# A fused attention and feed-forward kernel: the first pair's squares moved to ACT and DVE, the second pair's moments split, the first weight transfer tied to the first scale

## The chip, the cores and the metric

One core of one Trainium2 chip. The metric is the device time of one execution in microseconds (us). TensorE is written PE, VectorE DVE, ScalarE ACT, GpSimd POOL, SyncE SP. The "span" of a trace is the time from its first to its last event; it is some 1.8 us shorter than the timed figure of the same execution.

## The reference, cut to what matters

```python
q_n = q / (norm(q) + 1e-6); k_n = k / (norm(k) + 1e-6)   # 8 batches, 12 heads, 448 x 64, fp32
attn = softmax(q_n @ k_n.T / 0.1)
x = (attn @ v)                                           # regrouped to 3584 x 768
h = x @ w_in                                             # W1: 768 x 2048
out = (h * cos(h)) @ w_out                               # W2: 2048 x 768
```

## The kernel before

Work runs in pairs of heads, six pairs to a batch; pairs and batches are counted from 1 here. For each pair: load q and k; get the row norms; scale; transpose on PE and copy (DVE); scores (PE); exponentials (ACT, four of 896 columns); products with the values (PE). After six pairs the first projection, cosine (ACT), product (DVE) and second projection follow. The program is recorded operation by operation, a list scheduler gives each engine an order, and semaphores are put in afterwards. So a small edit can move many instructions.

The row norms come in two ways. Letters in `PLAN["sq"]`, one entry for each of the first six pairs, choose:

```python
PLAN = {
    "sq": ["BA", "BA", "P", "BP", "P", "P"],   # B: moments on DVE, mended by A(CT) or P(OOL)
    "scale": ["DD", "P", "P", "P", "P", "P"],  # without B: squares, by the named engine(s)
}
...
    BEHIND = ("sq0.2", "sq0.2")
...
            if how[0] == "B":
                moments(u, p, how)        # 16 bn_stats of 64 columns, a mend, a short row sum (L752)
            else:
                square(u, p, how, heads)  # ACT (L728), DVE (L730) or POOL (L732), to bf16
                reduce(u, p, heads)       # one row sum of 1024 columns on DVE (L761)
            rnorm(u, p, p + 1)            # ln and exp on ACT (L789, L792)
            scale(u, p, PLAN["scale"][UP * u + p])   # L800
...
    load_w1(0)                            # POOL issues the two halves of W1: the transfer casts
    load_w1(1)
...
    for x, y in enumerate(BEHIND):
        P.order_only(find(y), find("W1.%d" % x))
```

Labels read `sq0.2` = squares of group 0 (six heads), third pair. Two buffers each hold six heads of q and k (`raw`) and of v (`vin`); loads for a later group wait until an earlier group's scales or copies have freed the buffer. The third group's loads (heads 1 to 6 of the second batch, pairs 7 to 9) go out in this way between 11 and 17 us in the kernel before, the fourth group's at 37, the fifth's (heads 1 to 6 of the third batch) at 57. The texts on record of the experiments count heads from 0 ("heads 6 to 11" are heads 7 to 12 here), their "second batch's last query" is that of the third group, and they call the cosine a sine.

## Time and profile before

| | |
|---|---|
| time, three executions | 427.87 us median, 427.61 to 428.27 |
| span of the trace | 424.1 us |
| first exponential; 13th; end of the 24th | 12.60; 24.64; 34.49 us |
| first cosine of the first batch | 40.04 us |
| W1, first half: issue, landing | 9.89, 26.85 us |

The stretches 8 to 14, 15 to 25 and 25 to 40 us of the kernel before (columns: stretch, its length, then busy time and instruction count of PE, PEld, DVE, ACT, POOL, then clock, DMA share and GB/s):

```profile
8.00:14.00 6.00, 5.14 (x33) 2.20 (x32) 5.84 (x17) 2.08 (x7) 4.89 (x4) 1.00 1.12 293
15.00:25.00 10.00, 8.82 (x121) 4.93 (x118) 8.07 (x16) 9.64 (x17) 9.77 (x8) 1.00 1.12 236
25.00:40.00 15.00, 14.87 (x212) 9.44 (x210) 12.94 (x55) 10.77 (x13) 6.13 (x11) 1.00 1.13 229
```

Two things are to be seen. The last column is never low: the DMA engines are full (the column before it, their share, stands at 1.12 to 1.13), at 293 GB/s with loads alone and at some 235 with W1 beside them. And PE, which is what bounds the kernel (busy for 416.4 of 424.1 us), is idle for only 0.13 us of 15 from 25 us on.

### The profile page before, as it was taken

Reading aid. Unit: us, or ns where it says so; the run is one execution under the profiler, and the core shown is the slowest. Engines: PE = TensorE matmul, PEld = TensorE weight load, DVE = VectorE, ACT = ScalarE, POOL = GpSimd, SP = SyncE. Lnnn points to the kernel's source line nnn. Section 1 sums busy time; section 2 is a strip of 40 time slices with the busy share of each in tenths; the row PEclk is TensorE's granted clock in tenths of the full one; section 3 lists DMA queues with packets and bytes.
Section 4 is the critical chain, followed back from the end, with each engine's and each line's share of the span. In section 5 each row is a group of like instructions: output and inputs, shape, how many; then the busy total and the mean of one; then the engine's idle time right before and its main releaser. Section 6 shows DMA issues by size and latency. Waiting matters only on the chain.

```text
span 424.1 us, 8975 instructions
## 1 busy us (share of the span) xinstructions
PE 416.4 (98%) x3794; PEld 230.6 (54%) x3794; DVE 221.9 (52%) x403; ACT 259.4 (61%) x316; POOL 194.5 (46%) x147
## 2 busy tenths in 40 slices
PE   8899999999999999999999999999999999999997
PEld 3356555555555555555555555555555555555555
DVE  6978876465626359224663358434582344234422
ACT  2895498874777557674577547775567745754400
POOL 3872589645575556925277055751369100000000
PEclk9999999999999999999999999999999999999999
DMA  8999997496299794779529791388935501220033
GB/s 238 262 234 227 241 260 174 97 265 178 72 219 218 170 250 108 137 133 276 135 65 160 192 273 49 82 158 207 195 87 130 121 0 36 64 60 0 2 91 97
DMA packets 92008, 63.19 MB, mean 149 GB/s; under 512 B 52288, under 2 KB 86976, under 8 KB 91968
## 3 DMA queue, kind: packets, MB, share of 16 engines
q1 hardware_dynamic: 87312, 55.47, 56.4%
q0 software_dynamic: 3680, 6.29, 8.0%
q10 hardware_dynamic: 976, 0.86, 0.7%
q8 instruction: 30, 0.49, 0.5%
q14 instruction: 10, 0.08, 0.1%
HBM read 45.61 MB, written 11.01 MB: 134 GB/s over the span
## 4 chain that ended last, share of the span: by engine, by line
PE 85%; ACT 10%; DVE 2%; DMA 1%; POOL 1%; issue 1%; ACTq 0%; POOLq 0%
PE PP L979 28%; PE SC L924 25%; PE AV L873 11%; PE AV L924 9%; ACT PX L855 6%; PE SC L850 5%; PE AV L850 3%; ACT L645 2%; ACT cosb L944 2%; PE SC L979 1%; PE AV L979 1%; DVE st L741 1%; DMA raw<-in_k_dram 1%; DVE qks L800 1%; PE PP L903 1%; PE PP L924 1%
## 5 line engine op out<-in xcount | busy, mean ns | idle before, releaser
L979 PE MATMUL PP<-W,gT 128*128 128x384 bf16 x832 | 152.3, 327 | 0.0
L855 ACT ACTIVATE PX<-SC 112x896 bf16<-112x896 f32 x144 | 123.3, 916 | 2.4 <-PE SC L850 2.2
L732 POOL TENSOR_TENSOR sq<-raw 112x1024 bf16<-112x1024 f32 x39 | 73.2, 1893 | 87.8 <-DMA raw<-in_q_dram 58.9
L924 PE MATMUL SC<-xT,W 128*128 128x448 bf16 x552 | 109.0, 353 | 0.4 <-DVE rcp L883 0.4
L979 PEld LDWEIGHTS PP<-W,gT 128*128 128x128 bf16 x832 | 74.2, 98 | 61.6 <-issue 18.7
L800 POOL TENSOR_TENSOR qks<-raw,rn 112x1024 bf16<-112x1024 f32 x47 | 88.1, 1901 | 8.2 <-ACT rn L792 7.9
L944 ACT ACTIVATE cosb<-SC,cst 128x896 f32<-128x896 f32 x46 | 46.2, 1007 | 58.0 <-PE SC L924 55.4
L946 DVE TENSOR_TENSOR gT<-SC,cosb 128x896 bf16<-128x896 f32 x46 | 50.1, 1091 | 57.2 <-ACT cosb L944 57.1
L924 PEld LDWEIGHTS SC<-xT,W 128*128 128x128 bf16 x552 | 53.3, 98 | 49.2 <-issue 0.5
L855 ACT ACTIVATE PX<-AV 112x896 bf16<-112x896 f32 x48 | 44.0, 917 | 48.9 <-PE AV L850 48.9
L873 PEld LDWEIGHTS AV<-va,PX 112*128 112x128 bf16 x1536 | 49.6, 97 | 14.6 <-ACT PX L855 11.4
L873 PE MATMUL AV<-va,PX 112*128 112x65 bf16 x1536 | 56.0, 194 | 0.5
L988 DVE COPY osb<-PP 128x384 f32<-128x384 f32 x52 | 28.8, 554 | 46.3 <-PE PP L979 46.3
L761 DVE TENSOR_REDUCE n<-sq 112x16 f32<-112x1024 bf16 x42 | 50.0, 1210 | 1.5 <-POOL sq L732 1.5
L850 PE MATMUL SC<-qkT 64*128 64x448 bf16 x288 | 43.0, 353 | 1.8 <-DVE qkT L840 0.7
L924 PE MATMUL AV<-xT,W 128*128 128x448 bf16 x204 | 41.5, 353 | 0.0
L883 DVE RECIPROCAL rcp<-AV 112x8 f32<-112x8 f32 x48 | 9.9, 205 | 56.4 <-PE AV L873 56.3
L884 DVE TENSOR_TENSOR xs<-AV,rcp 112x512 bf16<-112x512 f32 x48 | 33.2, 691 | 2.1
L710 POOL CAST va<-vin 112x1536 bf16<-112x1536 f32 x14 | 20.4, 1463 | 27.5 <-PE AV L873 19.5
L924 PEld LDWEIGHTS AV<-xT,W 128*128 128x128 bf16 x204 | 19.9, 98 | 18.5
L944 ACT ACTIVATE cosb<-AV,cst 128x896 f32<-128x896 f32 x17 | 17.1, 1007 | 20.3 <-PE AV L924 20.2
L946 DVE TENSOR_TENSOR gT<-AV,cosb 128x896 bf16<-128x896 f32 x17 | 18.5, 1089 | 15.8 <-ACT cosb L944 15.6
(54 smaller groups left out, 184.7 us busy)
## 6 DMA issues: line engine op xcount, KB each, us to landing
vin<-in_v_dram SPq DMA_DIRECT2D x16, 672.0 KB, 9.1
raw<-in_k_dram SPq DMA_DIRECT2D x12, 672.0 KB, 7.6
raw<-in_q_dram SPq DMA_DIRECT2D x12, 672.0 KB, 9.3
W<-in_moe_w_in_dram POOLq DMA_DIRECT2D x2, 1536.0 KB, 21.4
W<-in_moe_w_out_dram POOLq DMA_DIRECT2D x4, 768.0 KB, 21.3
raw<-in_k_dram SPq DMA_DIRECT2D x12, 224.0 KB, 7.0
out_dram<-osb SPq DMA_DIRECT2D x7, 336.0 KB, 2.8
out_dram<-osb SPq DMA_DIRECT2D x8, 288.0 KB, 3.1
```

Source lines behind the costliest of these rows:

```text
L732: pool(lambda e, x=x, y=y: e.tensor_tensor(y, x, x, ALU.mult), src_, dst, 0.1 + n * 1.78e-3, label=name)
L761: dve(lambda e, o=o, hs=hs: e.tensor_reduce(out=n2v[i][:, o, :], in_=sqv[p][:, hs[0] : hs[-1] + 1, :, :], axis=mybir.AxisListType.X, op=AL ...
L800: f = lambda e, s0=s0, s1=s1: e.tensor_tensor(qksv[i][:, p, s0:s1, :, :].rearrange("p s h d -> p h s d"), rawv[i][:, h, s0:s1, :], bass.AP ...
L850: t = e.matmul(bank[:, a, 0:S], qkT[k].ap()[r, NP * c : NP * c + 128], qkT[k].ap()[r, S : 2 * S], start=True, stop=True)
L855: act(lambda e: e.activation(PXv[j][:, c, 0 : 2 * S].rearrange("p (a s) -> p a s", a=2), bank[0:NP, :, 0:S], ACT.Exp, scale=1.0 / TAU), [n ...
L873: t = e.matmul(AVv[:, a, DV * x : DV * x + n], PXv[j][:, c, k : k + 128], vav[i][:, NJ * (2 * p + a) + c, 0:n], start=(c == 0), stop=(c == ...
L884: dve(lambda e: e.tensor_tensor(xsv[y].rearrange("p x h d -> p h x d"), AXv[:, :, :, 0:D], bass.AP(rcp[y], 0, [[NS, NP], [NJ, 2], [1, NJ], ...
L924: t = e.matmul(ph[:, a, 0:S], W1v[:, c, 128 * n : 128 * n + 128], xTv[b % 2][:, c, :], start=(c == 0), stop=(c == NKC - 1))
L944: act(lambda e, ph=ph, cz=cz: e.activation(cosv[cz], ph[:, :, 0:S], ACT.Sin, bias=cst.ap()[:, 0:1], scale=1.0), names(gi) + ["cst0"], [("c ...
L946: dve(lambda e, ph=ph, cz=cz, gi=gi: e.tensor_tensor(gTv[:, 2 * gi : 2 * gi + 2, S * (b % 2) : S * (b % 2) + S], ph[:, :, 0:S], cosv[cz], ...
L979: r = e.matmul(po[:, 0 : w1 - w0], gTv[:, y, col : col + 128], W2v[:, y, w0:w1], start=(y == 0), stop=(y == NF - 1))
L988: dve(lambda e, po=po, o=o, w0=w0, w1=w1: e.tensor_copy(osb[o].ap()[:, w0:w1], po[:, 0 : w1 - w0]), keys, [("osb", o, w0)], w1 - w0, label ...
```

## The change

The intent is an earlier first exponential: the first pair's norm should come sooner, and POOL should be silent while DVE scales that pair.

```diff
-    "sq": ["BA", "BA", "P", "BP", "P", "P"],
+    "sq": ["AD", "BA", "P", "BP", "P", "P"],
...
-    BEHIND = ("sq0.2", "sq0.2")
+    BEHIND = ('scale0.0', 'scale0.0')
...
     P.order_only(find("scale0.0"), find("red0.1"))
+    P.order_only(find("red0.0"), [o for o in P.ops if o.label == "bn0.1"][0])
+    P.order_only(find("qkT0"), find("bn0.1"))
...
-        P.order_only(find(y), find("W1.%d" % x))
+        y = find(y)
+        (P.order_only if y.eng == "POOL" else after)(*((y, find("W1.%d" % x)) if y.eng == "POOL" else (find("W1.%d" % x), y)))
...
+    P.order_only(find("X16"), find("load v u7"))
```

In what the scheduler makes of it, W1's first half goes out on POOL directly behind DVE's scales and ahead of pair 3's square; the second half goes out much later, behind pair 4's scale.

## The prediction

> **What bounds the kernel now.** I read the page first, then the chain of work that ended last in order of time, then the timelines of ScalarE (ACT), GpSimd (POOL) and VectorE (DVE) for the first 36 us, and the landing times of the first loads.
>
> The page's busy rows say that TensorE has nothing left over the whole span:
>
> ```profile
> PE 416.4 (98%) x3794; PEld 230.6 (54%) x3794; DVE 221.9 (52%) x403; ACT 259.4 (61%) x316; POOL 194.5 (46%) x147
> ```
>
> A change on DVE and POOL can therefore only win where the chain isn't on PE, and that is the start. The chain in order of time, cut to the start (start us, us, what):
>
> ```profile
> 0.74 3.37 DMA raw<-in_k_dram
> ...
> 4.14 3.14 DVE st L741 x24
> 7.28 0.12 DVE n L752
> 7.39 1.02 DVE st L741 x8
> 8.42 2.69 DVE qks L800 x2
> ...
> 12.84 1.91 POOL qks L800
> ...
> 24.73 3.23 ACT PX L855 x4
> 27.97 0.04 issue
> 28.01 0.36 PE SC L850 x2
> ...
> 33.80 1.62 PE SC L924 x8
> ```
>
> Up to 12.6 us the chain is the first pair's work: load k, moments (L741), row sums, scale (L800). From 12.6 to 28 it alternates between POOL's scale of the next pairs and ACT's exponentials (PX); from 28.01 on it is PE without holes, through the first projection (L924 from 33.80). So the change has to be priced by when ACT's 24 exponentials of the first six pairs run. ACT's timeline (start, us, engine, line, what):
>
> ```profile
> 12.60 0.92 ACT L855 ACTIVATE PX<-SC 112x896 bf16<-112x896 f32 x1
> 13.41 0.30 ACT L789 ACTIVATE lnn<-n,cst 112x16 f32<-112x16 f32 x1
> 13.74 0.21 ACT L792 ACTIVATE rn<-lnn 112x16 f32<-112x16 f32 x1
> 13.86 3.62 ACT L855 ACTIVATE PX<-SC 112x896 bf16<-112x896 f32 x4
> ...
> 24.18 0.31 ACT L789 ACTIVATE lnn<-n,cst 112x16 f32<-112x16 f32 x1
> 24.52 0.21 ACT L792 ACTIVATE rn<-lnn 112x16 f32<-112x16 f32 x1
> 24.64 9.85 ACT L855 ACTIVATE PX<-SC 112x896 bf16<-112x896 f32 x12
> ```
>
> ACT is full from 12.60 to 34.49: 24 exponentials at 9.85/12 = 0.82 us and four pairs of small ln/exp of about 0.5 us. What feeds them comes from POOL, which has one hole of 1.05 us, before 12.84:
>
> ```profile
> 8.05 1.89 POOL L732 TENSOR_TENSOR sq<-raw 112x1024 bf16<-112x1024 f32 x1 [6.57 <-DMA raw<-in_q_dram]
> 9.89 1.90 POOL L1012 DMA_DIRECT2D W<-in_moe_w_in_dram  x2
> 12.84 3.76 POOL L800 TENSOR_TENSOR qks<-raw,rn 112x1024 bf16<-112x1024 f32 x2 [1.05 <-ACT rn L792]
> ```
>
> And the first pair's two scales on DVE, minimum/median/maximum in ns:
>
> ```profile
> L800 DVE TENSOR_TENSOR qks<-raw,rn x2: 676/1416/2156, 8.3 to 10.4; 112x512 bf16<-112x512 f32 x2
> ```
>
> Two equal instructions, 2.16 and 0.68 us: the long one started at 8.34, inside POOL's square (8.05 to 9.94), and ended 0.56 us after it.
>
> [...] a 1024-column square takes 1.08 us here. [...] here W1's first half lands 17.0 us after its issue.
>
> **The change, part by part.** Pairs are counted from 1.
>
> *Pair 1's squares.* Removed: 16 DVE moment instructions (0.127 us from start to start), ACT's fix of the moments (0.25) and a row sum of 0.20. Added: one ACT square of 512 columns[...], one DVE square of 512 columns (0.68, the free L800) and one row sum over 1024 (1.21, the L761 row). k lands at 4.12 and q at 4.38 (3.4 and 3.6 us after issue). DVE squares 4.41 to 5.09[...], the row sum runs 5.11 to 6.32. Before, the row sum ended at 7.40, because k of pair 2 was put in front of it. ln and exp (0.31 + 0.21 + hand-overs) give the norm at 6.9 in place of 7.98. Eight moments of pair 2, now ordered behind the row sum, hold DVE until 7.3; so the scales start at 7.3, not 8.34: 1.0 us won.
>
> *The first W1 issue now waits for the scale.* It stands ahead of pair 3's square in POOL's order, so POOL is silent while DVE scales: 0.68 + 0.60 to 8.55, where before it was 11.10. [...] In all 2.5 us are won on pair 1's scale.
>
> *Pair 2's moments split around the copies.* The q half (1.0 us) now stands between the two copies of pair 1's transposes, so the second copy ends at 10.2 (before 11.95) and the first exponential can start at about 10.9: 1.7 us won.
>
> *What gives it back.* In the changed order POOL does, one after the other from 8.65: issue W1 (1.06), square pair 3 (1.89, to 11.6), scale pair 2, scale pair 3. DVE's row sum of pair 3 (1.21) cannot end before 12.8, and ACT, which works in order, has pair 3's ln and exp directly behind the first exponential. The second exponential then starts at 12.85 + 0.55 = 13.4, where before it was 13.86. ACT stands idle 1.0 us and only 0.45 of the 1.7 stay. Next gate: the scales of pairs 2 and 3 end at 11.6 + 3.75 = 15.35 (before 16.6), the moment fix of pair 4 at 16.0, its norm at 16.75. With that norm out of the way the second exponential of pair 2 starts at 17.55, before 18.08: 0.5. Last gate: POOL squares pair 5 (17.85), scales pair 4 (19.7), issues the second W1 (20.65, this one came before everything else until now), squares pair 6 (22.5); row sum to 23.75, norm to 24.25. ACT reaches this point at 23.7. The twelve last exponentials start at 24.25, before 24.64: 0.4.
>
> *Sum.* The exponentials end 0.4 us earlier, PE behind them the same, since its order from the first projection on is the old one but for one matmul moved forward. No later term of the diff adds work. 427.87 - 0.4, so 427.4.
>
> **The rivals.** *A: the whole 1.7 us arrive.* [...] Against it: POOL carries the same 17.5 us of work from 8.05 to 26.66 with a hole of 1.05; it now starts 0.6 later, so it can't finish pair 6's scale much earlier than now. If ACT's wait on pair 3 is shorter than I think, 426.2. *B: W1 or W2 arrive late.* The second W1 issue moves from 10.9 to 19.7. Against it: the first half lands at 26.8 now and the second queues behind it on the same queue; it is first needed at 43.98, and lands at 36.7 today. W2's last quarter is tighter: landing 57.4, and PE waited 0.2 us for it. If that transfer doesn't move forward, it takes back some 0.2 of the 0.4; with a real delay the time is 427.9 to 428.5. *C: the rearranged order of later batches costs or wins something.* The scheduler has moved a few score and output matmuls between 55 and 120 us. PE is full there, so I give it 0.3 us either way.
>
> **Range and chances.** The middle is 0.4 us won. The lower end, 426.3, is rival A nearly whole; the upper end, 428.2, is the gain eaten by B and C. Two per cent would be 8.6 us, five times the whole idle start that the change touches, and a loss of that size would need a weight transfer late by as much. Faster or slower by 2%: 1% each.
>
> **What would show it.** Right, step by step: both DVE scales of pair 1 near 0.68 us and over by about 8.6; the first exponential at 10.9 and a hole of about 1 us on ACT behind it, ended by pair 3's row sum; the second exponential near 13.4; the twelve last exponentials from about 24.25; the first long run of L924 near 33.4. Wrong: no hole behind the first exponential (then rival A), a PE wait for W at 44 or 57 us that grows (rival B), or a start that is 0.4 earlier at 34 us and an end that isn't (rival C).

The sum of the prediction was 427.87 − 0.4, so 427.4 us. Two of its terms are cut: the time of ACT's 512-column square of pair 1 and its end (nothing hung on it; in the trace of after it took 0.63 us), and the mechanism to which the 1.5 us of the first scale was put down. The 1.5 us itself is measured, 2.16 less 0.68 in the trace of before, and with the 1.0 us of the earlier start it makes the 2.5 that the text goes on with (8.55 against 11.10); that the 1.5 would go was the author's estimate.

## More of the kernel before

DVE's timeline of before in the stretch that will matter (start, us, engine, line, what):

```profile
35.97 1.10 DVE L741 BATCH_NORM_STATS2 st<-raw 112x6 f32<-112x64 f32 x8
36.98 0.19 DVE L883 RECIPROCAL rcp<-AV 112x8 f32<-112x8 f32 x1
37.21 0.69 DVE L884 TENSOR_TENSOR xs<-AV,rcp 112x512 bf16<-112x512 f32 x1
37.82 1.10 DVE L741 BATCH_NORM_STATS2 st<-raw 112x6 f32<-112x64 f32 x8
```

The second batch's moments (L741) stand between the row scales of the first batch's output (L884), in order, with no idle time in square brackets: their loads are just there. The landing of the values of heads 7 to 12, one of the loads that W1 meets (the row, then issue to landing):

```profile
L698 SPq DMA_DIRECT2D vin<-in_v_dram x1: 1347/1347/1347, 6.6 to 6.6; - x1
...
DMA to landing us min/median/max: 12.6/12.6/12.6
```

## The result and the profile after

| | before | after |
|---|---|---|
| time, median (range), 6 executions each | 428.07 us (426.40 to 429.09) | 428.30 us (427.27 to 429.25) |
| span of the trace | 424.1 | 426.3 |
| ratio after/before, 95% interval | | 1.0008, 0.9984 to 1.0032 |

A ratio here is the mean time of one kernel's fast runs over that of the other's of the same rounds, so it is not quite the ratio of the medians quoted. The 428.30 lies 0.1 us above the range that was predicted, and 0.9 above its middle.

The busy row of the page after hardly differs from that of before:

```profile
PE 416.3 (98%) x3790; PEld 229.7 (54%) x3790; DVE 220.4 (52%) x388; ACT 260.1 (61%) x316; POOL 194.7 (46%) x147
```

The front is as it was meant to be. First pair 1's scales, from the view of that line, then ACT's timeline:

```profile
L800 DVE TENSOR_TENSOR qks<-raw,rn x2: 674/679/684, 7.7 to 8.2; 112x512 bf16<-112x512 f32 x2
```

```profile
11.28 0.90 ACT L855 ACTIVATE PX<-SC 112x896 bf16<-112x896 f32 x1
12.93 0.31 ACT L789 ACTIVATE lnn<-n,cst 112x16 f32<-112x16 f32 x1 [0.75 <-DVE n L761]
13.26 0.22 ACT L792 ACTIVATE rn<-lnn 112x16 f32<-112x16 f32 x1
13.39 2.51 ACT L855 ACTIVATE PX<-SC 112x896 bf16<-112x896 f32 x3
...
24.44 3.32 ACT L855 ACTIVATE PX<-SC 112x896 bf16<-112x896 f32 x4
27.96 6.69 ACT L855 ACTIVATE PX<-SC 112x896 bf16<-112x896 f32 x8 [0.20 <-PE SC L850]
...
41.86 1.01 ACT L944 ACTIVATE cosb<-SC,cst 128x896 f32<-128x896 f32 x1 [5.90 <-PE SC L924]
```

Both scales take 0.68 us; the first exponential starts at 11.28 (before 12.60); the hole behind it is 0.75 us and is ended by pair 3's row sum; the 13th exponential starts at 24.44 (before 24.64). But then there is a new wait for PE of 0.20: the 17th exponential, the first of pair 5, starts at 27.96, as in before (24.64 and four steps of 0.82, about 27.9). The 24th exponential ends at 34.65 (before 34.49), and the first cosine comes at 41.86, 1.8 us later than before. PE's holes after 26 us name the place:

```profile
31.41 0.37 PE L903 MATMUL PP<-ident,xs 112*128 112x112 bf16 x4 [0.25 <-DVE xT L907]
39.96 0.37 PE L903 MATMUL PP<-ident,xs 112*128 112x112 bf16 x4 [1.09 <-DVE xs L884]
```

Before has no such line between 26 and 44 us. DVE, which PE waits for, waits for loads (compare the four lines of before):

```profile
32.34 1.11 DVE L741 BATCH_NORM_STATS2 st<-raw 112x6 f32<-112x64 f32 x8 [0.98 <-DMA raw<-in_q_dram]
...
37.95 1.11 DVE L741 BATCH_NORM_STATS2 st<-raw 112x6 f32<-112x64 f32 x8 [1.50 <-DMA raw<-in_q_dram]
...
39.21 0.69 DVE L884 TENSOR_TENSOR xs<-AV,rcp 112x512 bf16<-112x512 f32 x1
...
42.90 1.11 DVE L741 BATCH_NORM_STATS2 st<-raw 112x6 f32<-112x64 f32 x8 [1.00 <-DMA raw<-in_q_dram]
```

And the chain of work that leads to the fifth group's loads, in order of time, answers the chain shown for before, which had no transfer in it after the first load (the chains of two later traces of before do hold one each, of 28.86 us of W2 and of 11.95 us of q, so this is no mark of the kernel):

```profile
18.05 1.87 POOL qks L800
19.93 2.19 SPq L686
22.12 0.04 issue
22.16 20.71 DMA raw<-in_q_dram
42.88 0.02 issue
42.90 0.05 DVE st L741
...
54.85 3.77 POOL qks L800 x2
...
59.07 10.90 DMA raw<-in_q_dram
```

One q load of the second batch takes 20.7 us; DVE's moments, POOL's norms and scales and the next load hang on it. The values of heads 7 to 12 show the same:

```profile
L698 SPq DMA_DIRECT2D vin<-in_v_dram x1: 1283/1283/1283, 7.0 to 7.0; - x1
...
DMA to landing us min/median/max: 19.3/19.3/19.3
```

19.3 us from issue to landing in place of 12.6. Two causes are possible: W1's first packet moves at 14.81 us rather than 15.37, ahead of more of these loads; or the loads of this one execution were slow from the start, as the stretch 8 to 14 us suggests (before: 293 GB/s):

```profile
8.00:14.00 6.00, 4.67 (x34) 1.87 (x33) 5.68 (x25) 2.62 (x7) 5.27 (x4) 1.00 1.13 259
25.00:40.00 15.00, 13.56 (x198) 8.23 (x197) 11.36 (x46) 10.74 (x13) 7.47 (x18) 1.00 1.12 236
```

### The profile page after: what moved, and what is told of

It is laid out like the page before. It is cut to its first block, busy times and chain, and to the rows that moved or that the text cites. A ratio compares the mean times of both kernels' runs of the same rounds, so it can differ in the third digit from the quotient of the medians.

```text
span 426.3 us, 8957 instructions
## 1 busy us (share of the span) xinstructions
PE 416.3 (98%) x3790; PEld 229.7 (54%) x3790; DVE 220.4 (52%) x388; ACT 260.1 (61%) x316; POOL 194.7 (46%) x147
## 4 chain that ended last, share of the span: by engine, by line
PE 76%; DMA 7%; ACT 7%; POOL 4%; issue 2%; DVE 2%; SPq 1%; ACTq 0%; POOLq 0%; DVEq 0%
PE PP L979 26%; PE SC L924 22%; PE AV L873 10%; PE AV L924 8%; DMA raw<-in_q_dram 7%; PE SC L850 4%; ACT PX L855 3%; PE AV L850 3%; ACT L645 2%; POOL qks L800 2%; ACT cosb L944 2%; PE SC L979 1%; PE AV L979 1%; DVE gT L946 1%; POOL sq L732 1%
## 5 line engine op out<-in xcount | busy, mean ns | idle before, releaser
L924 PE MATMUL SC<-xT,W 128*128 128x448 bf16 x552 | 109.0, 352 | 0.2 <-DVE xT L907 0.2
L924 PEld LDWEIGHTS SC<-xT,W 128*128 128x128 bf16 x552 | 53.3, 98 | 49.1 <-DVE xT L907 0.6
L873 PEld LDWEIGHTS AV<-va,PX 112*128 112x128 bf16 x1536 | 49.5, 97 | 14.9 <-ACT PX L855 11.4
L873 PE MATMUL AV<-va,PX 112*128 112x65 bf16 x1536 | 55.7, 193 | 0.6
L761 DVE TENSOR_REDUCE n<-sq 112x16 f32<-112x1024 bf16 x43 | 51.2, 1211 | 2.9 <-POOL sq L732 2.4
L924 PE MATMUL AV<-xT,W 128*128 128x448 bf16 x204 | 41.5, 352 | 0.0
L710 POOL CAST va<-vin 112x1536 bf16<-112x1536 f32 x14 | 20.5, 1465 | 23.4 <-PE AV L873 19.4
L924 PEld LDWEIGHTS AV<-xT,W 128*128 128x128 bf16 x204 | 19.9, 98 | 18.5
L944 ACT ACTIVATE cosb<-AV,cst 128x896 f32<-128x896 f32 x17 | 17.1, 1008 | 19.4 <-PE AV L924 19.3
## 6 DMA issues: line engine op xcount, KB each, us to landing
W<-in_moe_w_in_dram POOLq DMA_DIRECT2D x2, 1536.0 KB, 17.1
```

The costliest lines, as they stand in the source:

```text
L761: dve(lambda e, o=o, hs=hs: e.tensor_reduce(out=n2v[i][:, o, :], in_=sqv[p][:, hs[0] : hs[-1] + 1, :, :], axis=mybir.AxisListType.X, op=AL ...
L873: t = e.matmul(AVv[:, a, DV * x : DV * x + n], PXv[j][:, c, k : k + 128], vav[i][:, NJ * (2 * p + a) + c, 0:n], start=(c == 0), stop=(c == ...
L924: t = e.matmul(ph[:, a, 0:S], W1v[:, c, 128 * n : 128 * n + 128], xTv[b % 2][:, c, :], start=(c == 0), stop=(c == NKC - 1))
L944: act(lambda e, ph=ph, cz=cz: e.activation(cosv[cz], ph[:, :, 0:S], ACT.Sin, bias=cst.ap()[:, 0:1], scale=1.0), names(gi) + ["cst0"], [("c ...
```

## The experiments

Eighteen runs were made, some of unchanged kernels. **Theory 1**: the change's early start of W1 takes bandwidth of the DMA from the loads that DVE needs next, and so takes back the gain of the front. **Theory 2**: the front's gain is lost whatever W1 does, because PE or POOL have no room behind it. **Theory 3**: what differs is the execution, not the kernel.

In some experiments ("frozen order") the scheduler is not asked again: an operation is put directly behind another in the finished order, and all else keeps its place.

```python
    P.arrange()
    def ops(label): return [o for o in P.ops if o.label == label]
    def put(o, y, later=1e-4): o.start = y.start + later
```

n1 and n2, whose front starts later, are not in the table. Read its columns so: q1, GB/s of the loads from 8 to 14 us (the queue of SP and ACT alone, counted in the trace's packet records; in f3 W1 is already under way in this stretch); W, first packet of W1; v, landing of the values of heads 7 to 12; q2, landing of the last q of the third group; E, end of the 24th exponential; cos, first cosine; S − E, span less E; q3, landing of the fifth group's q.

| run | q1 | W | v | q2 | E | cos | q3 | span | S − E |
|---|---|---|---|---|---|---|---|---|---|
| before | 293 | 15.4 | 19.2 | 37.8 | 34.5 | 40.0 | 67.6 | 424.1 | 389.6 |
| r1_before_again | 281 | 15.3 | 20.8 | 38.4 | 34.4 | 39.9 | 67.7 | 424.2 | 389.8 |
| t1_before | 251 | 16.3 | 23.1 | 40.6 | 34.7 | 40.3 | 69.4 | 426.3 | 391.6 |
| after | 259 | 14.8 | 26.3 | 42.9 | 34.7 | 41.9 | 70.0 | 426.3 | 391.6 |
| r2_after_again | 261 | 14.9 | 25.2 | 41.7 | 34.8 | 40.7 | 68.9 | 425.5 | 390.7 |
| t2_after | 243 | 15.1 | 27.2 | 44.0 | 35.2 | 43.0 | 70.7 | 427.9 | 392.7 |
| r4_before_ad | 291 | 16.0 | 17.8 | 36.0 | 34.6 | 40.0 | 68.4 | 424.8 | 390.2 |
| r3_after_w1_sq | 287 | 16.1 | 19.4 | 37.3 | 34.6 | 39.9 | 69.2 | 425.6 | 391.0 |
| e3_ad_right_score | 274 | 16.1 | 19.2 | 37.6 | 34.7 | 40.0 | 68.1 | 425.3 | 390.6 |
| f1_after_w1_sq | 247 | 16.8 | 22.3 | 39.8 | 35.3 | 40.8 | 69.3 | 425.6 | 390.3 |
| c1_after_w1_late | 280 | 19.0 | 17.8 | 31.0 | 35.7 | 41.1 | 69.0 | 425.4 | 389.7 |
| c2_after_w1_late_u3 | 259 | 19.7 | 19.0 | 34.4 | 35.8 | 41.2 | 70.0 | 426.6 | 390.8 |
| c3_before_w1_late | 258 | 20.9 | 19.0 | 31.0 | 37.5 | 43.0 | 70.9 | 427.4 | 389.9 |
| f3_before_w1_early | 233 | 13.5 | 31.0 | 46.3 | 40.8 | 46.3 | 70.0 | 430.7 | 389.9 |
| f2_after_late | 247 | 15.1 | 27.3 | 43.8 | 35.3 | 41.4 | 70.3 | 426.8 | 391.5 |
| e1_ad_scores_first | 276 | 16.6 | 19.3 | 37.3 | 36.4 | 41.8 | 69.8 | 427.1 | 390.7 |
| e2_after_w1_scores | 246 | 17.1 | 22.7 | 40.3 | 36.2 | 41.7 | 70.4 | 426.8 | 390.6 |
| f4_before_extra | 292 | 15.2 | 20.0 | 38.4 | 34.3 | 39.9 | 71.4 | 427.8 | 393.5 |

### Is there a difference between the two kernels?

Both kernels were run again unchanged, first with five rounds, later for one look.

> The kernel before, unchanged, for a second profile. Theory A (the earlier W1 issue is what pushed the loads back): as in the first profile of before, values of heads 6 to 11 land near 19 us, the last q load of the second batch near 38 us, the first sine starts near 40.0 us, span near 424. Theory B (the two profiles differ by the run's own DMA speed): this profile can show the early loads at some 250 GB/s in place of 300 between 10 and 14 us, and then the same late landings as the changed kernel had (values near 22 to 26 us, last q near 40 to 43), and a span near 426.

> The changed kernel, unchanged, for a second profile. Theory A: late landings again (values of heads 6 to 11 near 26 us, last q near 43 us), PE hole of about 1 us near 40 us, first sine near 41.9 us. Theory B: with a fast start of the DMAs the landings come some 3 to 4 us earlier, the hole shrinks to nothing and the first sine starts near 39.7 us. Time against before between 0.997 and 1.003 by either.

> A third trace of the kernel before, to tell whether the speed of the loads between 4 and 14 us belongs to the kernel or to the execution. If to the kernel: again 280 to 300 GB/s between 10 and 14 us and a span near 424.2. If to the execution: it can be 240 to 250, and the span is then 426 or more though no instruction differs.

> A third trace of the changed kernel. If the slow early loads belong to the kernel: again 245 to 250 GB/s between 10 and 14 us and a span of 425.5 or more. If to the execution: it can be near 290, and then values of heads 6 to 11 land near 21 us, the first sine starts near 40.2 us and the span is 424.0 to 424.8.

Measured: before again 428.11 us (425.98 to 429.47), ratio 1.0008 (0.9987 to 1.0030) to before itself; after again 427.75 (427.33 to 428.86), ratio 0.9998 (0.9981 to 1.0016). The third trace of before has this line:

```profile
8.00:14.00 6.00, 5.34 (x36) 2.49 (x33) 5.81 (x17) 2.00 (x7) 4.66 (x4) 1.00 1.12 251
```

251 GB/s, not 293, for the same program, and its span is 426.3 like that of after. So the 2.2 us between the first two traces need no difference between the kernels: Theory 3 alone can make them. With all timed rounds together, before has a mean of 428.31 us (70 executions, 425.98 to 431.60, standard deviation 1.11). These rounds ran on several chips, and before's mean went from 427.82 to 428.94 from one set of rounds to the next; after was timed in two sets only. In those two, after has 428.07 (12 executions, deviation 0.62) and before 427.86 (17, deviation 0.80): a difference of +0.21 with a standard error of 0.26 (the root of 0.80²/17 + 0.62²/12). The predicted −0.4 is more than two standard errors off; no difference at all is not excluded. The first two traced executions of before, 425.95 and 425.98 us, were its two fastest of all, so one must not read a loss of 2 us from the traces.

It is not shown that the speed of the loads has nothing to do with the change: of the nine traces in the table that were made from the kernel before, six have early loads above 270 GB/s, of the nine made from the changed kernel two (r3 and c1). t1_before shows only that they can be slow without it.

At like speed of the loads something is left over, though. Of t1_before (251) and after (259), after has the values 3.2 us later and the first cosine 1.6 us later, and DVE's three waits for loads, which t1_before has not. That is for Theory 1. (r2_after_again, 261, is 2.0 and 0.4 us later than t1_before.) But it does not show in the span of these two, 426.3 both. Where it is given back can be seen on PE in t1_before:

```profile
59.06 0.82 PE L979 MATMUL PP<-W,gT 128*128 128x384 bf16 x4 [1.12 <-DMA W<-in_moe_w_out_dram]
```

Before, with slow loads, comes early to W2's last quarter and waits 1.12 us for it. After comes later and doesn't wait (it has one hole of 0.39 us between 44 and 100 us).

### The front alone, and what it leads to

r4_before_ad is the kernel before with only this edit:

```diff
-    "sq": ["BA", "BA", "P", "BP", "P", "P"],
+    "sq": ["AD", "BA", "P", "BP", "P", "P"],
```

r3_after_w1_sq is the changed kernel with `BEHIND = ("sq0.2", "sq0.2")` again. The scheduler was asked again in both, and in both it also put W1's second half behind pair 4's scale (19.8 us), as in the change. r3 keeps the other ordering lines of the diff; none of those was tested alone.

> The kernel before with the first pair's squares on ACT and DVE alone; W1 issues and orders as before. Both theories: norm of pair 1 near 7.1 us in place of 7.98, so the scales start near 7.7; POOL's square of pair 3 meets the second of them, which takes over 1 us. First exponential near 11.3 us, W1 issue near 9.9 to 10.5. Theory A: landings as in before, 0 to 0.5 us faster than before. Theory B: as the run's DMAs go, within 0.7 us of before.

> The changed kernel with W1's issues behind pair 3's square again, as before the change; the other parts stay. W1's first half is then issued near 10.5 us in place of 8.6. Theory A: some 1.5 us more of the SP queue at 250 to 300 GB/s in place of 75, so values of heads 6 to 11 land 4 us or more earlier than in the changed kernel, no PE hole near 40 us, and 0.5 to 1.5 us faster than the changed kernel. Theory B: no difference outside the noise of about 0.7 us.

Measured: r4 427.64 us, ratio 0.9999 (0.9974 to 1.0025); r3 428.85, ratio 1.0019 (0.9999 to 1.0040). Both start the first exponential at 11.14 and 10.93 and the 13th at 23.09 and 23.03, 1.6 us before the kernel before. None of it reaches the 24th exponential. Theory 1 had expected r3 to be 0.5 to 1.5 us faster than the changed kernel; in the same rounds its mean was 0.9 us longer (standard error 0.4). That putting W1 back would give the time back is thus not borne out.

r4's scales were a surprise too: its record expected the second of them to take over 1 us beside POOL's square. Both took 0.68 us, from 7.60 to 8.88, and it was POOL's square, which started after the first of them, that took 2.83 us rather than 1.89:

```profile
7.80 2.83 POOL L732 TENSOR_TENSOR sq<-raw 112x1024 bf16<-112x1024 f32 x1 [6.32 <-DMA raw<-in_q_dram]
```

So pair 1's scales are fast here without moving W1: the tie of W1 was not needed for them. Here is r4's ACT:

```profile
24.43 2.51 ACT L855 ACTIVATE PX<-SC 112x896 bf16<-112x896 f32 x3
27.88 6.76 ACT L855 ACTIVATE PX<-SC 112x896 bf16<-112x896 f32 x8 [0.94 <-PE SC L850]
```

ACT waits 0.94 us for pair 5's scores. In PE's order pair 6's transposes stand ahead of these scores. Is this order the cause, or has PE no room in any order? Two runs moved, in r4's order, one score matmul pair of pair 5 in front of the last eight value products of pair 3 and of those transposes, all else frozen:

```diff
+    put(ops("SC4.0")[0], ops("AV2")[-1], -1e-4)    # e1_ad_scores_first
+    put(ops("SC4.1")[0], ops("AV2")[-1], -1e-4)    # e3_ad_right_score
```

> The kernel before with only the square half of the change, and on TensorE the first scores of pair 5 moved ahead of the last eight products with the values of pair 3 and of pair 6's transposes. If the order loses the lead: pair 5's exponentials start at 26.9 to 27.1 us rather than 27.9, the 24th ends at 33.7 to 34.1 rather than 34.6, first sine 39.2 to 39.5 rather than 40.0, span 423.5 to 424.3 with fast early loads. If TensorE has no room in any order: pair 5's exponentials start early, but the 24th still ends at 34.4 or later, or the first sine stays at 39.9 to 40.1, and the span stays at 424.5 to 425.5.

> The kernel before with only the square half of the change, and the scores that ScalarE reads first of pair 5 moved ahead of the last eight products with the values of pair 3 and of pair 6's transposes. If the order of TensorE loses the lead: the wait ahead of pair 5's exponentials falls from 0.94 to 0.3 us or less, the 24th exponential ends 0.6 us or more earlier at like start (like-for-like: from the 13th exponential on at most 11.0 us, against 11.55), first sine 0.3 to 0.6 earlier at like start, span 423.5 to 424.5 with fast early loads. If TensorE has no room: the wait falls but the later exponentials wait instead, first sine and span as in the run with only the square half: from the 24th exponential's end less than 5.4 us is not reached, first sine 39.9 or later at the same start.

e1 was a mistake (and the granted clock fell to 0.79 from 8 to 14 us in its trace, so that its front isn't to be compared): ACT reads chunk 4.1 first, and chunk 4.0, which was moved, had to wait for pair 4's last exponential (over at 28.08) to free its PSUM bank, with PE behind it (idle for 0.42 us, until 28.14). The wait grew to 1.50 us, the 24th exponential ended at 36.40, the span was 427.1 and the time 428.94, ratio 1.0001 (0.9969 to 1.0033). e3 moves the right chunk. Its ACT timeline:

```profile
27.15 1.73 ACT L855 ACTIVATE PX<-SC 112x896 bf16<-112x896 f32 x2 [0.46 <-PE AV L873]
29.34 2.53 ACT L855 ACTIVATE PX<-SC 112x896 bf16<-112x896 f32 x3 [0.46 <-PE SC L850]
32.12 2.53 ACT L855 ACTIVATE PX<-SC 112x896 bf16<-112x896 f32 x3 [0.25 <-PE SC L850]
...
40.02 1.91 ACT L944 ACTIVATE cosb<-SC,cst 128x896 f32<-128x896 f32 x2 [4.06 <-PE SC L924]
```

The first wait is halved and two new ones appear: 0.46 + 0.46 + 0.25 = 1.17 us. Its 13th exponential started at 22.84, 0.25 ahead of r4's, yet the 24th ended at 34.66 and the first cosine came at 40.02, as in r4 (34.64, 40.01) and in before (34.49, 40.04). This order is not the cause; waits for PE only move. Time 428.01, ratio 1.0002 (0.9970 to 1.0033). The bound is not PE alone: W2's issue, which follows POOL's last scale of the first batch, begins at 26.66 us in before, 26.46 in after and 26.44 in r4, and pair 6's work on PE can begin only when that scale is done. From there to the first cosine PE is all but full in before and in r4 (no hole listed, and one of 0.15 us).

r4 shows a second place where a lead is lost. POOL's timeline, first of before, then of r4:

```profile
53.01 3.77 POOL L800 TENSOR_TENSOR qks<-raw,rn 112x1024 bf16<-112x1024 f32 x2
56.73 3.75 POOL L732 TENSOR_TENSOR sq<-raw 112x1024 bf16<-112x1024 f32 x2
```

```profile
50.86 3.76 POOL L800 TENSOR_TENSOR qks<-raw,rn 112x1024 bf16<-112x1024 f32 x2
55.66 3.75 POOL L732 TENSOR_TENSOR sq<-raw 112x1024 bf16<-112x1024 f32 x2 [1.04 <-DMA raw<-in_q_dram]
```

r4's POOL is 2.2 us ahead and waits for the fourth group's q load, which lands at 55.59 (before 55.46).

### When W1 starts

f1 is the changed kernel in frozen order with only W1's two issues put back behind pair 3's square. f3 is the dose in the other direction, the kernel before with W1 issued 2.6 us earlier, at 7.26. f2 leaves W1 where the change has it and moves the waiting moments away from DVE's row scales.

```diff
+    put(ops("W1.0")[0], ops("sq0.2")[0])                    # f1_after_w1_sq
+    put(ops("W1.1")[0], ops("sq0.2")[0], 2e-4)
 ...
+    w0, w1, s = ops("W1.0")[0], ops("W1.1")[0], ops("sq0.2")[0]   # f3_before_w1_early
+    for w in (w0, w1): w.deps = [d for d in w.deps if d[0] is not s]
+    w0.deps.append((ops("bs0.0")[0], True))
+    put(w0, s, -2e-4); put(w1, s, -1e-4)
 ...
+    for n, o in enumerate(ops("bn2.1")): put(o, ops("xT5")[0], 1e-4 * (n + 1))   # f2_after_late
+    put(ops("bn2.2")[0], ops("g0.2")[0])
```

> The changed kernel's own order of instructions, frozen, with both W1 issues alone moved back behind pair 3's square. Transfer theory: W1's first packet comes near 16 us in place of 14.8, values of heads 6 to 11 land near 18 to 20 us (25.2 and 26.3 in two traces of the changed kernel), the last q of the second batch by 38.5 (41.7 and 42.9), the PE hole at 40 us is gone and the first sine starts near 40.2 (40.7 and 41.9). Compute theory (the lateness comes from the rearranged order of DVE and PE): landings move but the first sine stays near 40.7 to 41.9 and the span at 425.5 or more.

> The kernel before, order frozen, with both W1 issues alone moved ahead: released by the first pair's moment fix at 6.6 us, in place of 9.9. A larger dose of what the change does. Transfer theory: W1's first packet 3 us earlier, near 12.2; from there the SP queue gets 75 GB/s in place of 290, so it lacks 3 x 0.215 MB and values of heads 6 to 11 land 8 us later, near 27 to 28, the last q of the second batch near 45; span 2 us or more longer, 426 to 429. Compute theory: span within 0.7 of 424.2, as no instruction of DVE, ACT or PE moves.

> The changed kernel's order frozen, only DVE's moments of pair 8 moved behind the last copy of the first batch, and the first of pair 9 behind the third product with the cosine. Nothing on DVE in front of the first projection then waits for late loads. If the late loads cost their time through DVE's order: landings as late as before (last q near 42 us), no PE hole near 40, first sine near 40.0 and third sine near 42.2 in place of 43.9 to 45.0, span lower by 0.5 to 1.5. If they cost it through the stream itself (W2 and the next loads): first sine earlier but the span unchanged at 425.5 to 426.3.

f3 gave 432.53 us and a span of 430.7, 6.6 above before's. Its values landed at 31.0 us rather than 19.2, and DVE, and PE behind it, stood still once for long, until they were there:

```profile
30.97 0.69 DVE L706 TENSOR_REDUCE va<-vin 112x512 bf16<-112x512 f32 x1 [4.85 <-DMA vin<-in_v_dram]
...
32.24 0.72 PE L832 MATMUL PP<-ident,qks 112*128 112x112 bf16 x8 [3.92 <-DVE qkT L840]
```

So an earlier W1 did great harm here (part of it by the clock, which was granted at 0.89 from 25 to 40 us: after that stop, at 33.76, 16 matmuls of L873 took 1.06 us, where 16 of them at 27.03 had taken 0.66). f1 gave 428.67, ratio 1.0001 (0.9950 to 1.0051). Its early loads were slow too (247) and the values came later than the 18 to 20 us expected, but at 22.3 us, not 25 to 27, and no PE hole of 1 us came ahead of the first cosine; the way from the 24th exponential to that cosine took 5.4 us, not 5.9 to 7.9 as in the three traces of after; in before it is 5.6, in t1_before too, slow loads or not. Its front, however, was later by W1's second issue on POOL (13th exponential 25.11). f2 gave 428.76, ratio 0.9995 (0.9951 to 1.0040): no gain in time. Its first cosine, expected near 40.0, came at 41.4, 1.6 us before t2's with about as slow loads (247 against 243), and then PE waited 0.92 us for POOL's scale at 57.33, where t2's does not.

The last three of this group start W1 later still, behind POOL's scale of pair 2. c1 and c2 are the changed kernel, c3 is the kernel before; c2 also lets the fourth group's loads go without W1's second half.

```diff
+    put(ops("W1.0")[0], ops("scale0.1")[0])                 # c1, c2 and c3
+    put(ops("W1.1")[0], ops("scale0.1")[0], 2e-4)           # c3 alone
 ...
+    ks = {id(o) for o in ops("W1.1")}                       # c2 alone
+    for o in ops("load u3 p0"): o.deps = [d for d in o.deps if id(d[0]) not in ks]
```

> The changed kernel with W1's first half issued behind POOL's first scale of pair 2, all else in its order. Theory (W1's early start delays the other loads): W1's first packet at 18 to 19 us rather than 14.8 to 15.1; values of heads 6 to 11 landed by 17 to 20 us rather than 25 to 27; last query of the second batch by 33 to 39 us rather than 42 to 44; first sine at 40.0 to 40.8 us rather than 40.7 to 43.0. Second exponential up to 1 us earlier, as the issue is out of the way of pair 3's square. Cost: W1's first half lands at about 30.5 us, PE's first matmuls on it may wait up to 1 us. Theory for the end (one saturated stream of loads): the span follows the landing of the query load of the fifth group as before and stays at 424.5 to 426.5. Rival (the early order of loads sets the end): span 423 to 424.

> As the run before, and the fourth group's loads do not wait for W1's second half. Last query of the second batch by 31 to 35 us; no idle time of DVE ahead of moments in 32 to 43 us; W1's second half a little later, 38 to 41 us, still ahead of its first use at about 44. W2's last quarter at 58 to 60 us, and PE may wait for it. One-stream theory: span 424.5 to 426.5; rival: 423 to 424.

> The kernel before with both halves of W1 issued behind POOL's scale of pair 2. If W1's start competes with the other loads, the values of heads 6 to 11 land by 16 to 18 us rather than 19 to 23, the second batch's last query by 33 to 37 us rather than 38 to 41. First exponential unchanged at 12.5. PE may wait up to 1 us for W1's first half at about 30 us. One-stream theory: span within 1 us of 424.1 to 426.3; rival: 1 us or more below 424.1.

Measured: c1 428.69, ratio 1.0006 (0.9984 to 1.0028); c2 428.16, 0.9998 (0.9977 to 1.0019); c3 429.58, 1.0029 (1.0008 to 1.0049), so c3 is slower by some 0.3% (both W1 issues, 1.9 us, now stand ahead of pair 3's scale, and the clock fell to 0.84 from 14 to 25 us). DVE in c1 no longer waits for any of the loads that it waited for in after:

```profile
37.24 1.10 DVE L741 BATCH_NORM_STATS2 st<-raw 112x6 f32<-112x64 f32 x8
...
39.09 1.10 DVE L741 BATCH_NORM_STATS2 st<-raw 112x6 f32<-112x64 f32 x8
...
41.10 1.10 DVE L741 BATCH_NORM_STATS2 st<-raw 112x6 f32<-112x64 f32 x8
```

The third group's last q lands at 31.0 us rather than 41.7 to 44.0. The table has the whole dose: among traces with slow early loads (233 to 261), the values land at 31.0 us, at 25.2 to 27.3, at 22.3 to 23.1 and at 19.0 as W1's first packet comes at 13.5, at 14.8 to 15.1, at 16.3 to 17.1 and at 19.7 to 20.9. And with that packet at 15.2 us or later the way from the 24th exponential to the first cosine takes 5.4 to 5.6 us at any speed of the loads; at 14.8 to 15.1 it takes 5.9 to 7.9. (f3, at 13.5, stands still ahead of E already; n2, not in the table, takes 5.4 with the packet at 14.7, but its front is over 1 us later.) This half of Theory 1, that W1's start sets when the loads land and what DVE and PE wait, is shown by interventions. The other half, that this is what takes back the time, is not. S − E cannot show it: it is low in c1 and c3, but also in f3 (389.9), where W1 is earliest; in all three E itself is late. And the time does not follow, because each issue of W1 holds POOL wherever it stands (for 0.85 to 1.06 us in before, after and c1). c1's POOL:

```profile
13.49 1.06 POOL L1012 DMA_DIRECT2D W<-in_moe_w_in_dram  x1
14.57 1.93 POOL L800 TENSOR_TENSOR qks<-raw,rn 112x1024 bf16<-112x1024 f32 x1
```

It now stands ahead of pair 3's scale. The 13th exponential starts at 25.48 (after 24.44), E is 35.7, and the 0.5 us or more won between E and the first cosine is lost in front. I had expected a first cosine of 40.0 to 40.8 and got 41.1; I had left out the 1.06 us. c2 loses a further 1.59 us of PE to W2's last quarter, landing at 60.4 rather than 58.2 (c1) or 57.4 (before).

e2_after_w1_scores was to be the version that beats both: W1's first half one step later (behind pair 3's square), the second as in the change, and the score move of e1.

> The changed kernel with W1's first half issued behind pair 3's square rather than ahead of it (second half as in the change), and the same order of pair 5's scores. Theory: first exponential 11.3, second 12.9 to 13.3, 13th 24.4 to 24.7, W1's first packet 16 to 17 us, values of heads 6 to 11 by 19 to 22 us, last query of the second batch by 35 to 39 us, first sine 39.8 to 40.3, span 424 to 425.5: the kernel before again, not better. A version that beats both would show a span under 423.6.

It carried e1's mistake (ACT again waits 1.50 us), and gave 428.57, ratio 1.0001 (0.9967 to 1.0035), span 426.8. Nothing follows from it but that W1's first packet at 17.1 us brought the values at 22.7 even with loads of 246 GB/s.

### The stream of loads

f4 adds 672 KB of useless loads to the kernel before, behind the second batch's loads; n1 and n2 take 768 KB away from before and after: W2's last quarter is not loaded but zeroed on POOL (wrong, relative error 0.499).

```diff
+    for n, o in enumerate((2, 3)):                          # f4: two loads of 336 KB into output buffers not yet in use
+        x = P.op("SP", lambda e, o=o: [e.dma_start(osb[o]..., src(k, 6, 0, 3))], ..., label="extra")
+        put(x, ops("load u2 p2")[0], 1e-4 * (n + 1))
 ...
+    x = ops("W2.3")[0]                                      # n1, n2
+    x.dma, x.deps, x.fn = None, [], (lambda e: e.memset(W2v[:, 12:16, :]..., 0.0))
```

> The kernel before, order frozen, with one useless load of 672 KB added to the SP queue behind the second batch's loads. Transfer theory (the loads of the first 65 us are one stream that moves some 235 GB/s all the time): everything behind it lands 2 to 3 us later, the next-but-one q load near 70 in place of 67.6, span 2 to 3 us longer. Compute theory: span within 0.7 of 424.2.

> The kernel before, order frozen; W2's last quarter is set to zero by GpSimd at the start and not loaded (wrong result on purpose). It takes 768 KB (1.5 MB of reads) out of the stream behind 52 us. If the stream bounds the stretch from 53 to 90 us: the q load that landed at 67.6 lands 3 to 5 us earlier, no PE wait for W2 at 57.7, and the time falls by 0.5 to 1.5 us, no more, since PE has only some 1.3 us of holes behind 26 us. If not: no change.

> The same on the changed kernel. If the stream bounds the stretch from 53 to 90 us: what the changed kernel lost there against before (0.9 us between the last sine of the first batch and the first of the second) is gone, and the time falls by more than in the kernel before, 1.0 to 2.0 us; what it lost in front of 53 us stays. If the loss there comes from the changed order of instructions: it stays, and the time falls by no more than in the kernel before.

f4 took 429.62 us, span 427.8 against 424.1. Up to the first cosine it is before again (39.90 against 40.04), and then PE has holes that before has not:

```profile
58.71 0.82 PE L979 MATMUL PP<-W,gT 128*128 128x384 bf16 x4 [1.15 <-DMA W<-in_moe_w_out_dram]
64.68 1.12 PE L873 MATMUL AV<-va,PX 112*128 112x65 bf16 x32 [1.36 <-POOL va L710]
```

The queue had no slack for these 672 KB: the fifth group's q lands 3.8 us later than before's and the span is 3.7 us longer (2 to 3 expected; one look).

n1 and n2 are inconclusive. The memset of 2.8 us on POOL at the very start pushed the first exponential from 12.60 to 14.73 in n1 (in its chain the matmuls on zeros with which PE opens go on until 13.16, when the first pair's transposes begin; in before these begin at 10.55), and two microseconds of it are still there at the first cosine (42.19). They took 428.93, ratio 1.0022 (0.9986 to 1.0058), and 428.68, ratio 1.0003 (0.9973 to 1.0034). I had expected a gain from the lighter stream and none came.

## Why the prediction was right or wrong

**Right: the scales.** Two of 0.68 us each, none of 2.16 as in before, over at 8.9 us (predicted 8.6). W1's issue began at 8.64, before the second scale ended: it waited for the first alone, where the prediction had it wait for both. In before the long one started inside POOL's square (8.34, in 8.05 to 9.94); here, with that square not begun before 9.72, 2.16 us became 0.68. In r4, where DVE started first (7.60, POOL's square at 7.80), the scales took 0.68 us too, and POOL's square had the delay (2.83 rather than 1.89). By what mechanism the two meet is not shown.

**Right: the first exponentials.** The first at 11.28 (predicted 10.9; the first pair's loads landed 0.2 to 0.3 us later than in the trace of before), a hole of 0.75 (predicted 1.0) ended by pair 3's row sum, the second at 13.39 (13.4; its scores had ended at 11.14, but ACT took pair 3's ln and exp first, in order, as the prediction had it), the 13th at 24.44 (24.25). The exact hit at 13.39 has some luck in it: DVE was 0.3 us later than predicted, but W1's issue, which leads to pair 3's row sum, did not wait for all of DVE's work. Rival A, the whole 1.7 us arriving, fell for the reason that the prediction gave.

**Wrong: "The exponentials end 0.4 us earlier, PE behind them the same".** This is the step that failed: of the gain at the 13th exponential, 0.2 us to before's first trace, nothing was left four exponentials later, because the next one waited for PE (27.96 against about 27.9). The first long run of L924, predicted near 33.4, came at 33.99 (before 33.73). The 24th ended at 34.65 to 35.15 in three traces of after, and at 34.35 to 34.73 in three of before. r4, r3 and e3 show why no lead of the front arrives there: with 1.6 to 1.8 us of lead at the 13th exponential the 24th still ends at 34.6 to 34.7, the first cosine stays at 39.9 to 40.0, and moving the score that was in the way only moves the wait. The prediction had both facts in hand, POOL's unchanged sum of work and PE without holes from 28.01 us, and used the first against rival A only, not against its own 0.4. In this stretch a lead of ACT was worth nothing, because PE had no room behind it (in before it is idle for 0.13 us of the 15 from 25 us on).

**Wrong: "No later term of the diff adds work".** No work was added, but an order was changed: W1 went out 1.25 us earlier (8.64 against 9.89), and its first packet moved 0.2 to 1.5 us earlier (14.8 to 15.1 us in after, 15.3 to 16.3 in before; in the first traces it is 6.2 and 5.5 us after the start of the issue on POOL, and what of this is the load on the DMA engines no run here shows). From then on the loads of SP, at 293 (before) and 259 GB/s (after) from 8 to 14 us, get some 75 GB/s and W1 some 157 in the first traces of both kernels. The packet records of both traces show how: from 16 to 24 us each of the two queues sends about 155 packets in 2 us, of 1 KB for the loads and 2 KB for W1. The prediction looked at W1's side alone. What landed late was the other side. No rival named this: rival B asked whether W1 or W2 come late, and rival C looked to 55 to 120 us and needed a start that is earlier at 34 us, which there was not. f3, f1 and c1 show by intervention that the landings follow W1's start. In the three traces of after the waits that this puts on DVE go with a loss of 0.4 to 2.3 us between the 24th exponential and the first cosine (5.9 to 7.9 against 5.6); in the timed executions no part of it can be told from noise.

**Mis-sized: the range.** It started from the median of three executions that spread by 0.7 us and was made of the rivals alone, without that spread. Single executions of the same kernel spread from 426.0 to 431.6, so even a median of six moves by several tenths, and the kernel before gave 428.07 in the rounds of the result. Measured against that, the result's own rounds say +0.3 us with an interval of −0.7 to +1.4 (the ratio and its interval, less 1, times 428), and its rounds together with those of r2 +0.21, with a standard error of 0.26.

**What the time is made of, then.** Front: 0.3 to 0.5 us at the 13th exponential at like speed of the loads (24.44 to 24.59 against t1_before's 24.89), gone by the 24th. Loads: 0.4 to 2.3 us lost at the first cosine; t1_before, which comes there earlier, lost 1.12 us later on, waiting for W2's last quarter. Net: nothing that 12 against 17 executions can tell from zero.

**What stays open.** In 15 of the 18 experiments' traces, and in the first traces of both kernels, the span is 356.3 to 357.3 us more than the landing of the fifth group's q load; f3 (360.7), n1 (358.8) and n2 (360.4) are not so. f4 shows that delaying this load delays the end, n1 and n2 show that it is not the only gate; which gate takes over is not settled. Why early loads run at 251 to 293 GB/s from one execution of before to the next, at a clock of 1.00 and with spans 2.2 us apart, was not found, nor whether the change has a share in the 243 to 261 of after; no trace here shows the two kernels at fully equal load speed, and the size of Theory 1's share for after, as against its existence, remains an estimate. No version here beats both kernels: r4, at 427.64, has the lowest median but a ratio of 0.9999.

## What to carry to other kernels

An earlier start of one stage was worth here only what the next full engine could use: before counting a lead, look whether the engine that follows has any idle time between there and the end. The weight transfer that started earlier took its bandwidth from the loads beside it (some 75 GB/s were left to them), so ask which other transfers it will meet and who waits for those. And before a prediction of tenths of a microsecond, run the kernel often enough to know its spread.
